# An attention-and-gated-projection kernel whose instruction order a planner makes: new planner costs, an exclusion rule for VectorE and GpSimd, and a longer chosen list

## The chip, the cores and the metric

One core of one Trainium2 chip runs the whole problem in one launch. The metric is the time of one execution on the device, in microseconds, median of the runs shown. Five instruction queues matter: TensorE (PE, with its weight loads PEld), VectorE (DVE), ScalarE (ACT), GpSimd (POOL) and SyncE (SP), which here issues nearly all DMA transfers.

## What is computed

```python
def _attn_ref(q, k, v, omega):                  # q, k, v: 8 x 8 x 576 x 64, omega: 128 x 64
    scale = 1.0 / np.sqrt(np.sqrt(D))
    def phi(x):
        proj = np.einsum('bhsd,md->bhsm', x, omega)
        h = proj - np.sum(x * x, axis=-1, keepdims=True) / 2.0
        return np.exp(h - np.max(h, axis=-1, keepdims=True)) / np.sqrt(m)
    q_p, k_p = phi(q * scale), phi(k * scale)
    kv, z = np.einsum('bhsm,bhsd->bhmd', k_p, v), np.sum(k_p, axis=2)
    num = np.einsum('bhsm,bhmd->bhsd', q_p, kv)
    return num / (np.einsum('bhsm,bhm->bhs', q_p, z)[..., None] + 1e-06)

def _moe_ref(x, w_a, w_b, w_out):               # 4608 x 512, 512 x 1536 twice, 1536 x 512
    return ((x @ w_a) * (x @ w_b)) @ w_out      # x is the attention's output, heads side by side
```

## The kernel before

**Two kinds of work.** Attention is cut into 32 units, one for each batch entry and pair of heads. A unit multiplies its input X by omega (`four`, `eight`: PE lines L583, L603), takes row maxima on DVE (L654, L613), makes biases of them (L661, L662), runs exponentials on ACT (L667, L623), and then forms k'v (pkv), the normaliser and the result. The dense part runs in nine blocks of 512 tokens; its matmuls are written as three products of a high and a low half of each operand, so every operand is first split: a CAST makes the high half, a subtraction (`subber`, L408) the low one. Blocks 0 and 1 (`moe_block`, PE lines L1285 and L1093) use the weights as they are. From block 2 on (`moe_block7`, L1383) a form with seven products in place of eight is used; it needs sums of the weights (`weight_sums`, L1317 to L1326, on DVE).

**The first 300 us carry everything that happens once.** The inputs of the weights come as 64-bit numbers. Each of 36 pieces (`raw`) is turned into a 32-bit number by two ACT instructions (L450, L452) and one DVE instruction (L454), and then split by a CAST, which the planner may give to ACT or to DVE (`convert`), and a DVE subtraction. In the same stretch the first eight attention units run. The first four have a longer way of their own (`tok_tail`): transposes on PE (pq, L990), the products pkv (L1013) and pn (L1027), then on DVE rd (L1032, L1034), x32t (L1035) and tails (L1039), then transposes back on PE (px, L1046; pt, L1050), and a split into the x that the dense blocks read.

**GpSimd** sums the exponentials of a unit over the tokens (`z_sums`, L829: z and zs), in three pairs of additions per unit. DVE transposes and reduces the sums, SP takes them through DRAM into zb, and DVE divides (L895 to L907).

**What sets the order.** Nothing of it is written by hand. Each piece is a `g.op` with its engine or engines, a cost in ns, what it reads and writes, and a priority. `Graph.plan` replays the program by these costs with `run`, which each time starts the piece that can start first. From a replay `dues` works back to the latest time for each piece; the next replay takes DVE, ACT and POOL work by those due times. `CHOSEN` is a list of lists of seeds: in each replay `shifted` adds random delays, drawn from the seed that stands for that 15 us stretch (0: none), to the due times. The order of the last replay is the program's: five queues, each served strictly in order, and a choice of ACT or DVE for some copies. The planner's constants of interest: `BW` and `LANDING` give a transfer's time, `TURNS` the cost of PE changing between kinds of matmul, `PORT` lets half of the time that a DVE piece shares with GpSimd count as lost. `SP` issues cost 330 ns each.

Of the kernel before, what the change touches and what calls it, by code (L numbers as in the profile page):

```python
# [41 lines left out]
CFG = dict(PORT=0.5, EDF=("DVE", "ACT", "POOL"), STEP=15000, LOOK=60000, NOISE=(200, 600), CHOSEN=((448364,600862,0,0,820305,0,0,230255),), ZS=800, ZB=(300, 1600, 3600), ZD=(300, 1600, 3100), HQ=(1100, 2600, 3600), BACK2=(300, 1100, 2600), TW=(), XL=["v0", "v1", "Xt0", "ht2", "hq0"], OWR=["raw0", "raw1"], ONE=((7, 1),), SAFE=500, OWN=16, OWNU=(), HOLD=1000, TG=1, G4=4, WAIT=150, RAW=600, FAST=(0, 1, 2, 3), JOIN0=False, WARM=8, HROOM=["w0", "u1", "w1", "u2", "w2", "u3"], H=3, TURN=(7,), BACK=1500, AT=2, GATES=(-4, -1, 2, 5), SQPE=4, MARGIN=1200, LOAD=1100, SUMS=1000, NATS=(1, 2, 3), CONV=(28000, 2600))  # L42
# [19 lines left out]
class Graph:  # L62
# [3 lines left out]
    BW, LANDING = 330.0, 3400  # L66
    TURNS = {"fr": 190, "rf": 205, "fc": 145, "cf": 205, "rc": 250, "cr": 250}
# [13 lines left out]
    def op(self, eng, fn, r=(), w=(), prio=0, alloc=(), deps=(), margin=0, nbytes=0, at=0, land=0, late=(), fill=False, mode="f"):  # L81
# [5 lines left out]
        o.port = not any(b.ring in ("at", "ab", "o") for b, _ in r)  # L87
# [97 lines left out]
    def begin(self):  # L185
# [17 lines left out]
        self.ready, self.done, self.mode = {e: [] for e in self.ENGINES}, [], "f"  # L203
# [4 lines left out]
    def enter(self, o):  # L208

        t = 0  # L210
        for d in o.deps:
            same = d.eng.keys() == o.eng.keys() == {"PE"}
            t = max(t, d.start + 1, d.end + (0 if same else self.LAT + (150 if "PE" in d.eng else 0)) + (o.land or CFG["SAFE"] * (not o.margin) if d.bytes else 0) - (900 if o.late and o.late is not True and d in o.late else 0))
        o.need = max(t + o.margin, o.at)
        for e in o.eng:
            self.ready[e].append(o)

    def keep(self):

        return (len(self.done), dict(self.free), self.dma_free, list(self.left), {e: list(r) for e, r in self.ready.items()},  # L220
                {n: r["at"] for n, r in self.rings.items()}, dict(self.slots), self.mode)

    def back(self, kept):

        n, free, self.dma_free, left, ready, at, slots, self.mode = kept
# [4 lines left out]
        for name, k in at.items():  # L230
            self.rings[name]["at"] = k

    def run(self, until=1e12, due=None):

        free, ready, found = self.free, self.ready, {}
        while len(self.done) < len(self.ops):
            best = None
            for e in self.ENGINES:
                mine = None
                for o in ready[e]:  # L240
# [114 lines left out]
def pool2(n):  # L355
    return 250 + 2.19 * n
# [3 lines left out]
def tile_attention_moe(ctx: ExitStack, tc: tile.TileContext, kqt, kqtt, kqn, kqnt, vx, omst, idn, wab, wout, out):  # L360
# [69 lines left out]
    g.op({"PE": 2600}, nothing, r=[(zero, None)], w=[(none, None)], alloc=[none], prio=-6000)  # L430
# [37 lines left out]
    for n, (kind, i, w) in enumerate(units):  # L468
# [4 lines left out]
        g.op({"SP": 330}, dma(lambda raw=raw: raw.ap[:], lambda src=src: src), w=[(raw, None)], alloc=[raw], prio=pr - 600,  # L473
# [1136 lines left out]
```

## Time and profile before

| what | value |
|---|---|
| median of 3 runs | 1040.24 us (1039.75 to 1040.35) |
| profiled execution | 1038.92 us, its span 1037.1 us |
| PE busy | 1020.0 us (98%) |
| DVE, ACT, POOL busy | 803.8, 635.5, 117.2 us |
| TensorE clock granted | 0.999 of full speed over the span |
| DMA | 314.39 MB, mean 303 GB/s |

The span is cut into stages by what the program does: up to 50 us the first four attention units, to 300 us dense blocks 0 and 1 with all conversions, then the blocks of seven products. Busy time of PE counts from a matmul's start to its modelled end, and matmuls overlap: twelve of 128x512 follow each other about 0.23 us apart while each is listed at about 0.4 us. A pause of PE under some 0.16 us is therefore not seen as idle time.

### The profile page before, as it was taken

Reading aid. Unit: us, or ns where it says so; the run is one execution under the profiler, and the core shown is the slowest. Engines: PE = TensorE matmul, PEld = TensorE weight load, DVE = VectorE, ACT = ScalarE, POOL = GpSimd, SP = SyncE. Lnnn points to the kernel's source line nnn. Section 1 sums busy time; section 2 is a strip of 40 time slices with the busy share of each in tenths; the row PEclk is TensorE's granted clock in tenths of the full one; section 3 lists DMA queues with packets and bytes.
Section 4 is the critical chain, followed back from the end, with each engine's and each line's share of the span. In section 5 each row is a group of like instructions: output and inputs, shape, how many; then the busy total and the mean of one; then the engine's idle time right before and its main releaser. Section 6 shows DMA issues by size and latency. Waiting matters only on the chain.

```text
span 1037.1 us, 25617 instructions
## 1 busy us (share of the span) xinstructions
PE 1020.0 (98%) x9902; PEld 895.7 (86%) x9902; DVE 803.8 (78%) x1580; ACT 635.5 (61%) x1690; POOL 117.2 (11%) x181
## 2 busy tenths in 40 slices
PE   8899999999999999999999999999999999999998
PEld 6677777777788898989898889988989899999997
DVE  6999999999987687676776868677757467887545
ACT  7998787777676575667556666675555234444322
POOL 0133111111111111110201111111110000000000
PEclk9999999999999999999999999999999999999999
DMA  9977878999889898879898998988798899999991
GB/s 358 335 250 247 291 236 266 323 335 332 292 296 387 301 319 299 319 278 368 283 321 301 340 304 296 363 287 315 249 303 265 267 316 337 334 326 358 338 336 56
DMA packets 123658, 314.39 MB, mean 303 GB/s; under 512 B 17680, under 2 KB 40976, under 8 KB 123536
## 3 DMA queue, kind: packets, MB, share of 16 engines
q1 hardware_dynamic: 122656, 312.10, 86.6%
q8 instruction: 78, 1.28, 0.5%
q10 hardware_dynamic: 880, 0.66, 0.2%
q14 instruction: 44, 0.36, 0.1%
HBM read 255.52 MB, written 57.18 MB: 302 GB/s over the span
## 4 chain that ended last, share of the span: by engine, by line
PE 82%; DVE 12%; ACT 4%; issue 1%; DMA 1%; SPq 0%; DVEq 0%; ACTq 0%
PE p L1383 41%; PE o L1093 19%; PE o_P L1163 5%; PE pa L1285 3%; PE pb L1285 3%; PE pkv L876 3%; PE pm L950 2%; DVE sm L654 2%; PE ppk L603 2%; PE p L603 1%; DVE raw L454 1%; PE p L1163 1%; ACT hq L667 1%; DMA zb<-zdr 1%; ACT hk L667 1%
## 5 line engine op out<-in xcount | busy, mean ns | idle before, releaser
L1093 PE MATMUL o<-wo,ghl 128*128 128x512 f32 x1008 | 263.2, 396 | 0.4 <-DVE ghl L408 0.4
L1093 PEld LDWEIGHTS o<-wo,ghl 128*128 128x128 f32 x1008 | 178.6, 188 | 36.3 <-issue 4.1
L400 ACT COPY c<-p 128x512 f32<-128x512 f32 x150 | 87.4, 583 | 145.7 <-PE p L1383 137.8
L1395 DVE TENSOR_TENSOR c<-p,c 128x512 f32<-128x512 f32 x144 | 98.6, 685 | 71.1 <-PE p L1383 36.4
L1383 PE MATMUL p<-Sa,t 128*128 128x256 f32 x1008 | 133.4, 280 | 0.0
L1383 PEld LDWEIGHTS p<-Sa,t 128*128 128x128 f32 x1008 | 126.2, 188 | 2.3 <-issue 0.2
L829 POOL TENSOR_TENSOR z<-hk 128x256 f32<-128x256 f32 x56 | 48.0, 856 | 601.4 <-ACT hk L623 402.8
L1459 DVE TENSOR_TENSOR c<-c 128x512 f32<-128x512 f32 x82 | 57.8, 707 | 40.1 <-ACT c L400 39.4
L911 ACT ACTIVATE hq<-hq,dn 128x128 f32<-128x128 f32 x224 | 69.3, 390 | 13.5 <-DVE dn L907 13.0
L1285 PE MATMUL pa<-x,wa 128*128 128x512 f32 x288 | 74.4, 400 | 2.1 <-ACT a L400 1.1
L1285 PE MATMUL pb<-x,wb 128*128 128x512 f32 x288 | 72.3, 397 | 1.5 <-DVE a L1293 1.5
L1383 PE MATMUL p<-x,wa 128*128 128x256 f32 x504 | 73.7, 282 | 0.0
L1383 PE MATMUL p<-x,wb 128*128 128x256 f32 x504 | 73.2, 281 | 0.0
L1383 PEld LDWEIGHTS p<-x,wa 128*128 128x128 f32 x504 | 67.2, 188 | 3.3 <-ACT hk L400 0.6
L1383 PE MATMUL p<-Sb,t 128*128 128x256 f32 x504 | 68.4, 283 | 0.0
L1383 PEld LDWEIGHTS p<-x,t 128*128 128x128 f32 x504 | 64.7, 189 | 2.6
L1285 PEld LDWEIGHTS pa<-x,wa 128*128 128x128 f32 x288 | 52.6, 188 | 16.4 <-ACT a L400 1.9
L1383 PE MATMUL p<-Sb,bq 128*128 128x256 f32 x504 | 66.8, 282 | 0.0
L1285 PEld LDWEIGHTS pb<-x,wb 128*128 128x128 f32 x288 | 53.3, 188 | 15.5 <-DVE a L1293 2.8
L1383 PE MATMUL p<-x,t 128*128 128x256 f32 x504 | 66.7, 281 | 0.0
L1383 PEld LDWEIGHTS p<-Sb,bq 128*128 128x128 f32 x504 | 64.3, 189 | 2.4
L1383 PEld LDWEIGHTS p<-x,wb 128*128 128x128 f32 x504 | 65.4, 188 | 0.1
(217 smaller groups left out, 1983.9 us busy)
## 6 DMA issues: line engine op xcount, KB each, us to landing
t<-td SPq DMA_DIRECT2D x168, 512.0 KB
wo<-wod SPq DMA_DIRECT2D x96, 512.0 KB
bq<-bd SPq DMA_DIRECT2D x84, 256.0 KB
qdr<-qd SPq DMA_DIRECT2D x112, 160.0 KB
hq<-qdr SPq DMA_DIRECT2D x28, 640.0 KB
X<-in_kqt_dram SPq DMA_DIRECT2D x30, 512.0 KB
raw<-in_wab_dram SPq DMA_DIRECT2D x24, 512.0 KB
td<-ts SPq DMA_DIRECT2D x24, 512.0 KB
```

The source lines that it names most:

```text
L400: nc.scalar.copy(o(), i())
L603: nc.tensor.matmul(flat[c // 4][w]()[half, c % 4 * M:c % 4 * M + M], x()[rows, c * P + D * t:c * P + D * t + D], om.ap[rows], start=True, ...
L654: g.op({"DVE": dve(4 * M)}, lambda e, w=w, whole=whole: nc.vector.tensor_reduce(sm.ap[:, 0, w, sl], whole(), axis=X, op=ALU.max), r=held[w ...
L829: g.op({"POOL": pool2(n)}, lambda e: nc.gpsimd.tensor_tensor(o(), a(), c(), op=ALU.add), r=r, w=w, alloc=list(al), prio=pri, deps=zload[-1 ...
L876: nc.tensor.matmul(pkv.ap[D * j + d:D * j + d + Q, 0:M], vb.ap[:, vc, d:d + Q], c(), start=(n == 0), stop=(n == 4))
L911: g.op({"ACT": 392}, lambda e, c=c, src=src: nc.scalar.activation(hq.ap[:, c], src(), AF.Copy, scale=dn.ap[:, c:c + 1]), r=[sd, (dn, None) ...
L1093: nc.tensor.matmul(po.ap[:], ghl.ap[:, gi, t * P:(t + 1) * P], wo.ap[:, wi], start=(n == 0 and i == 0), stop=(n == NF - 1 and i == 2))
L1163: nc.tensor.matmul(pb.ap[:, t], A[0](ai)[:, t * P:(t + 1) * P], W[0](wi), start=begin and t == j == 0, stop=stop and t == 1 and j == 2)
L1285: nc.tensor.matmul(pb.ap[:], wt.ap[:, wi, c], xs[c].at(xi), start=(c == 0 and i == 0), stop=(c == NC4 - 1 and i == 2))
L1383: nc.tensor.matmul(pb.ap[:, w], W[w][0](wi, c), X[0](xi, c), start=fresh and n == w == 0, stop=n == 5, skip_group_check=True)
L1395: g.op({"DVE": dve(SM)}, lambda e: nc.vector.tensor_tensor(o.ap[:, q], pb.ap[:], C[y[0]].ap[:, y[1]], op=ALU.add), r=[(pb, 0), (pb, 1), (C ...
L1459: g.op({"DVE": dve(SM)}, lambda e, c=C[k]: nc.vector.tensor_tensor(c.ap[:, :, 1], c.ap[:, :, 1], c.ap[:, :, 0], op=ALU.mult), r=part, w=pa ...
```

## The change

No arithmetic is added or dropped, and every piece stays as it was, except that the two DVE instructions of rd become one piece of the planner. What changes is the planner:

- a DVE piece and a GpSimd piece now exclude each other: one that starts while the other engine holds the `lock` ends a whole duration (less `HOLD`) after the lock is released, on both engines. Pieces that only reduce or transpose (`port=False`) or read PSUM take no part. Before, DVE alone paid, half of the overlap.
- a transfer isn't issued while the modelled backlog is over `DEPTH` = 5600 ns; bandwidth is 395 instead of 330 bytes per ns, the fixed part 1000 + 1500 ns instead of 3400, an SP issue 450 ns instead of 330.
- `TURNS` are about half of what they were; a kind "h" (pkv and pn of the first units) is added.
- `CHOSEN` has six lists in place of one: five empty ones (five replays by due times without delays) and one of 38 entries, 10 of them not 0.

```diff
-CFG = dict(PORT=0.5, EDF=("DVE", "ACT", "POOL"), STEP=15000, LOOK=60000, NOISE=(200, 600), CHOSEN=((448364,600862,0,0,820305,0,0,230255),), ZS=800, ZB=(300, 1600, 3600), ZD=(300, 1600, 3100), HQ=(1100, 2600, 3600), BACK2=(300, 1100, 2600), TW=(), XL=["v0", "v1", "Xt0", "ht2", "hq0"], OWR=["raw0", "raw1"], ONE=((7, 1),), SAFE=500, OWN=16, OWNU=(), HOLD=1000, TG=1, G4=4, WAIT=150, RAW=600, FAST=(0, 1, 2, 3), JOIN0=False, WARM=8, HROOM=["w0", "u1", "w1", "u2", "w2", "u3"], H=3, TURN=(7,), BACK=1500, AT=2, GATES=(-4, -1, 2, 5), SQPE=4, MARGIN=1200, LOAD=1100, SUMS=1000, NATS=(1, 2, 3), CONV=(28000, 2600))
+CFG = dict(EDF=("DVE", "ACT", "POOL"), STEP=15000, LOOK=60000, NOISE=(200, 600), CHOSEN=((),(),(),(),(),(408745,0,244407,0,423927,388522,0,0,0,0,792291,441366,0,0,0,109497,0,0,0,0,41968,0,0,0,0,0,0,0,0,0,0,257791)), ZS=800, ZB=(300, 1600, 3600), ZD=(300, 1600, 3100), HQ=(1100, 2600, 3600), BACK2=(300, 1100, 2600), TW=(), XL=["v0", "v1", "Xt0", "ht2", "hq0"], OWR=["raw0", "raw1"], ONE=((7, 1),), SAFE=500, OWN=16, OWNU=(), HOLD=1000, TG=1, G4=4, WAIT=150, RAW=600, FAST=(0, 1, 2, 3), JOIN0=False, WARM=8, HROOM=["w0", "u1", "w1", "u2", "w2", "u3"], H=3, TURN=(7,), BACK=1500, AT=2, GATES=(-4, -1, 2, 5), SQPE=4, MARGIN=1200, LOAD=1100, SUMS=1000, NATS=(1, 2, 3), CONV=(28000, 2600))
...
-    BW, LANDING = 330.0, 3400
-    TURNS = {"fr": 190, "rf": 205, "fc": 145, "cf": 205, "rc": 250, "cr": 250}
+    BW, LEAD, LANDING, DEPTH, HOLD = 395.0, 1000, 1500, 5600, 130
+    TURNS = {"fr": 90, "rf": 95, "fc": 90, "cf": 75, "rc": 150, "cr": 150, "fh": 95, "hf": 100, "rh": 150, "hr": 100, "hc": 120, "ch": 120}
...
-        o.port = not any(b.ring in ("at", "ab", "o") for b, _ in r)
+        o.port = port and not any(b.ring in ("at", "ab", "o") for b, _ in r)
+        if not o.port and "ACT" in eng and any(b.ring in ("at", "ab", "o") for b, _ in r):
+            o.any = eng = dict(eng, ACT=eng["ACT"] - 30)
...
                     need = o.need if due is None else o.need + due[len(self.ops) + o.n]
+                    if o.bytes:
+                        need = max(need, self.dma_free - self.DEPTH)
...
-                begin = max(s, self.dma_free)
-                self.dma_free = begin + o.bytes / self.BW
+                begin = max(s + self.LEAD, self.dma_free)
+                self.dma_free = begin + max(60, o.bytes / self.BW) + (440 if o.eng[e] > 1000 else 0)
...
                 if e == "DVE" and o.port:
-                    o.end += CFG["PORT"] * max(0, min(o.end, free["POOL"]) - s)
+                    if s < self.lock["POOL"]:
+                        o.end = max(o.end, self.lock["POOL"] + o.eng[e] - self.HOLD)
+                    self.lock["DVE"] = o.end
+                elif e == "POOL":
+                    if s < self.lock["DVE"]:
+                        o.end = max(o.end, self.lock["DVE"] + o.eng[e] - self.HOLD)
+                    self.lock["POOL"] = o.end
...
-        g.op({"SP": 330}, dma(lambda raw=raw: raw.ap[:], lambda src=src: src), w=[(raw, None)], alloc=[raw], prio=pr - 600,
+        g.op({"SP": 450}, dma(lambda raw=raw: raw.ap[:], lambda src=src: src), w=[(raw, None)], alloc=[raw], prio=pr - 600,
...
-            g.op({"DVE": 150}, lambda e, o=o, pn=pn, rd=rd: nc.vector.tensor_scalar(rd.ap[:], pn.ap[:, :, o + D], EPS, None, op0=ALU.add),
-                 r=[(pn, None)], w=[(rd, None)], prio=pri)
-            g.op({"DVE": 165}, lambda e, rd=rd: nc.vector.reciprocal(rd.ap[:], rd.ap[:]), r=[(rd, None)], w=[(rd, None)], prio=pri)
+            def inv(e, pn=pn, rd=rd):
+                nc.vector.tensor_scalar(rd.ap[:], pn.ap[:, :, D], EPS, None, op0=ALU.add)
+                nc.vector.reciprocal(rd.ap[:], rd.ap[:])
+            g.op({"DVE": 470}, inv, r=[(pn, None)], w=[(rd, None)], prio=pri)
```

Lines of the changed kernel lie up to 11 below those of the kernel before (L654 is L665, L400 is L411, L1046 is L1057).

The first place is the head of DVE's queue: the maxima of the first three groups of unit 0 (sm, sme), out of ppk and ppq, and the biases made of them with the sums ps and pse that PE forms. Before:

```order
L654 TENSOR_REDUCE sm_0_183<-ppk_00_179 128x4
L654 TENSOR_REDUCE sm_0_183<-ppq_00_180 128x4
L654 TENSOR_REDUCE sme_0_212<-ppke_00_208 128x4
L654 TENSOR_REDUCE sme_0_212<-ppqe_00_209 128x4
L654 TENSOR_REDUCE sm_0_183<-ppk_04_239 128x4
L661 SCALAR_TENSOR_TENSOR sm_0_183<-sm_0_183,ps_00_265 128x2x4
L662 SCALAR_TENSOR_TENSOR sm_0_183<-ps_00_265,sm_0_183 128x2x4
```

And in the changed kernel:

```order
L665 TENSOR_REDUCE sm_0_169<-ppk_00_165 128x4
L665 TENSOR_REDUCE sm_0_169<-ppq_00_166 128x4
L672 SCALAR_TENSOR_TENSOR sm_0_169<-sm_0_169,ps_00_194 128x2x4
L673 SCALAR_TENSOR_TENSOR sm_0_169<-ps_00_194,sm_0_169 128x2x4
L665 TENSOR_REDUCE sme_0_211<-ppke_00_207 128x4
```

The first pair of biases moved ahead of three maxima. On PE the sums ps_00 moved likewise, to directly behind the first pp group; the next two sums (pse, ps_04) moved behind the pp group of unit 1.

The second place is PE's queue between pn and px of unit 1 (px_1), some 30 us into the program, where px waits for DVE's x32t. Before:

```order
L1027 MATMUL pn_11_652<-kvz_1_532,qT_1_564 64x66 x10
L990 MATMUL pq_20_669<-ident,hq_2_401 128x128 x3
L1013 MATMUL pkv_2_677<-v_2_169,hk_2_400 64x66 x8
L1013 MATMUL pkv_2_677<-v_2_169,htk_0_210 64x66 x2
L1013 MATMUL pkv_2_677<-v_2_169,hk_2_400 64x66 x8
L1013 MATMUL pkv_2_677<-v_2_169,htk_0_210 64x66 x2
L1046 MATMUL px_1_708<-ident,x32t_1_635 128x128 x4
```

And in the changed kernel:

```order
L1038 MATMUL pn_11_643<-kvz_1_523,qT_1_431 64x66 x10
L1024 MATMUL pkv_2_659<-v_2_199,hk_2_404 64x66 x8
L1024 MATMUL pkv_2_659<-v_2_199,htk_0_209 64x66 x2
L1024 MATMUL pkv_2_659<-v_2_199,hk_2_404 64x66 x8
L1024 MATMUL pkv_2_659<-v_2_199,htk_0_209 64x66 x2
L1001 MATMUL pq_20_693<-ident,hq_2_405 128x128 x3
L1061 MATMUL pt_1_698<-ident,tails_1_516 128x128
L1001 MATMUL pq_21_707<-ident,hq_2_405 128x128
L1001 MATMUL pq_21_707<-ident,htq_0_210 128x128
L1001 MATMUL pq_21_707<-ident,hq_2_405 128x128
L1001 MATMUL pq_22_713<-ident,hq_2_405 128x128 x3
L1038 MATMUL pn_20_726<-kvz_2_660,qT_2_694 64x66 x10
```

Behind these stands px_1 (x4): seven transposes and pn_20 of unit 2 moved between pn_11 and px_1.

The third place is ACT's queue ahead of the first copy of pa (a_0) of dense block 0. Before:

```order
L667 ACTIVATE hk_0_913<-ppqk_00_912,smk_0_914 128x128 x3
L400 COPY a_0_860<-pa_0_859 128x512
L450 ACTIVATE raw_520<-raw_520 128x512
L452 ACTIVATE raw_520<-raw_520 128x512
L400 CAST wo_1041<-raw_419 128x512
L400 CAST wa_1048<-raw_495 128x512
```

And in the changed kernel:

```order
L411 CAST wa_1035<-raw_470 128x512
L862 COPY zq_0_1030<-zq_0_1030 32x8 x3
L411 COPY k_1_0_1006<-pkv_0_1005 128x128
L411 CAST wb_1043<-raw_498 128x512
L461 ACTIVATE raw_552<-raw_552 128x512
L463 ACTIVATE raw_552<-raw_552 128x512
L463 ACTIVATE raw_519<-raw_519 128x512
L411 COPY a_0_950<-pa_0_949 128x512
```

Casts of weights and pieces of the second batch entry's first unit moved ahead of a_0. Over the whole program ACT's queue gains 19 copies and DVE's loses as many: 12 casts of weights net in the first 170 us, 8 net of 29 casts of ghl from c after 300 us, one output copy, and 2 casts of ghl from a the other way.

## Rows read from the trace of the kernel before

**Rows 1.** The page: busy time of each engine in us (share of the span, instructions), and the granted TensorE clock in 40 slices of the span, in tenths of full speed (9 is 90% or more).

```profile
PE 1020.0 (98%) x9902; PEld 895.7 (86%) x9902; DVE 803.8 (78%) x1580; ACT 635.5 (61%) x1690; POOL 117.2 (11%) x181
...
PEclk9999999999999999999999999999999999999999
```

**Rows 2.** Windows of the span, from and to in us: the length, then busy us of PE, PEld, DVE, ACT and POOL (with instructions), the granted clock, the busy share of the DMA engines and GB/s.

```profile
0.00:8.85 8.85, 7.85 (x120) 5.46 (x120) 3.53 (x9) 3.18 (x5) 0.94 (x10) 1.00 0.74 257
8.85:25.00 16.15, 13.62 (x283) 11.08 (x282) 12.95 (x35) 16.15 (x58) 0.20 (x1) 1.00 1.04 412
25.00:50.00 25.00, 20.19 (x351) 16.45 (x350) 24.09 (x62) 24.24 (x68) 1.55 (x3) 1.00 0.94 345
50.00:100.00 50.00, 48.92 (x410) 37.56 (x409) 49.51 (x98) 45.85 (x114) 18.06 (x18) 1.00 0.74 241
100.00:200.00 100.00, 98.47 (x853) 75.19 (x855) 97.93 (x198) 79.42 (x219) 18.62 (x24) 1.00 0.84 281
200.00:300.00 100.00, 98.91 (x899) 76.52 (x892) 96.76 (x186) 72.39 (x195) 16.00 (x24) 1.00 0.94 320
300.00:1025.00 725.00, 725.00 (x6945) 666.55 (x6946) 513.58 (x989) 394.25 (x1037) 61.87 (x102) 1.00 0.88 308
1025.00:1037.10 12.10, 7.05 (x60) 6.85 (x58) 5.43 (x9) 0.00 (x0) 0.00 (x0) 0.90 0.29 87
```

**Rows 3.** Whom PE waited for in the whole span, the five largest: us in total, times, the longest.

```profile
PE px L1046 <- DVE x32t L1035: 3.3, 4, 1.4
PE pb L1285 <- DVE a L1293: 1.5, 3, 0.6
PE pq L990 <- DVE rd L1032: 1.1, 1, 1.1
PE pa L1285 <- ACT a L400: 1.1, 2, 0.9
PE none L429 <- DVE zero L422: 1.0, 1, 1.0
```

**Rows 4.** The longest pieces of the chain that ended last (start and duration in us, what, its count).

```profile
89.48 2.79 PE pb L1285 x12
```

**Rows 5.** ACT in order of time, 0 to 12 us: start and duration in us, instruction, count, and in brackets the idle time before it and what ended it.

```profile
5.67 0.63 ACT L638 ACTIVATE x<-X 128x512 f32<-128x512 f32 x1 [0.16 <-DMA X<-in_kqt_dram]
8.85 1.14 ACT L667 ACTIVATE hk<-ppk,sm 128x128 f32<-128x128 f32 x4 [2.55 <-DVE sm L662]
```

**Rows 6.** DVE in order of time, 0 to 12 us, same columns.

```profile
6.60 0.68 DVE L654 TENSOR_REDUCE sme<-ppke 128x4 f32<-128x512 f32 x1
...
8.39 0.15 DVE L661 SCALAR_TENSOR_TENSOR sm<-sm,ps 128x8 f32<-128x8 f32 x1
```

**Rows 7.** PE in order of time, 0 to 12.5 us, same columns: the sums ps for the first group.

```profile
7.02 1.16 PE L643 MATMUL ps<-ind,x 128*128 128x128 f32 x8
```

**Rows 8.** The chain that ended last, in order of time, 0 to 60 us: four exponentials of a unit on ACT.

```profile
11.03 1.03 ACT hk L667 x4
```

**Rows 9.** PE in order of time, 26 to 48 us, same columns: pn of unit 1, transposes, and px of units 1 to 3 with their waits.

```profile
27.06 1.45 PE L1027 MATMUL pn<-kvz,qT 128*64 128x66 f32 x40
...
30.96 0.63 PE L1046 MATMUL px<-ident,x32t 128*128 128x128 f32 x4 [0.66 <-DVE x32t L1035]
...
31.53 0.27 PE L990 MATMUL pq<-ident,hq 128*128 128x128 f32 x1
31.64 0.27 PE L990 MATMUL pq<-ident,htq 128*128 128x128 f32 x1
...
37.09 0.66 PE L1046 MATMUL px<-ident,x32t 128*128 128x128 f32 x4 [1.11 <-DVE x32t L1035]
...
44.80 0.66 PE L1046 MATMUL px<-ident,x32t 128*128 128x128 f32 x4 [1.37 <-DVE x32t L1035]
```

**Rows 10.** DVE instructions that write or read wb: count, then shortest, median and longest in ns, first and last start in us, forms.

```profile
L402 DVE CAST wb<-raw x11: 410/420/964, 38.5 to 162.9; 128x512 fp32r<-128x512 f32 x11
```

**Rows 11.** ACT instructions that write or read wo, same columns.

```profile
L400 ACT CAST wo<-raw x8: 657/663/773, 52.1 to 168.7; 128x512 fp32r<-128x512 f32 x8
```

**Rows 12.** Line L454 of DVE (two inputs in SBUF), same columns.

```profile
L454 DVE SCALAR_TENSOR_TENSOR raw<-raw x36: 639/685/1611, 34.2 to 167.0; 128x512 int32<-128x512 int32 x36
```

**Rows 13.** Line L569 of DVE (a reduction, one input), same columns.

```profile
L569 DVE TENSOR_REDUCE sq<-natk x30: 630/678/687, 14.4 to 695.3; 128x8 f32<-128x512 f32 x30
```

**Rows 14.** Groups of DVE instructions from 50 to 250 us: count, then busy us and mean ns of one, then idle us before them.

```profile
L454 DVE SCALAR_TENSOR_TENSOR raw<-raw 128x512 int32<-128x512 int32 x31 | 23.4, 765 | 0.0
```

**Rows 15.** Groups of POOL instructions from 50 to 250 us, same columns.

```profile
L829 POOL TENSOR_TENSOR z<-hk 128x256 f32<-128x256 f32 x18 | 18.3, 1015 | 143.6 <-ACT hk L667 105.4 <-ACT hk L623 17.5 <-DVE wa L408 14.0
```

**Rows 16.** Line L829 of POOL over the whole span: count, then shortest, median and longest in ns, first and last start in us, forms.

```profile
L829 POOL TENSOR_TENSOR z<-hk x56: 722/742/2672, 49.5 to 770.5; 128x256 f32<-128x256 f32 x56
```

**Rows 17.** PE in order of time around an attention visit of the later stage: the last dense matmuls ahead of it, and the first matmul of the visit.

```profile
311.30 0.86 PE L1093 MATMUL o<-wo,ghl 128*128 128x512 f32 x3
312.09 0.32 PE L603 MATMUL ppk<-om,X 64*64 64x128 f32 x1
```

**Rows 18.** The page, costliest groups: the scalings of a unit by its divisor on ACT (count, busy us, mean ns).

```profile
L911 ACT ACTIVATE hq<-hq,dn 128x128 f32<-128x128 f32 x224 | 69.3, 390 | 13.5 <-DVE dn L907 13.0
```

More of the change, by code (lines that the diff above doesn't have):

```diff
@@ L79, in buf, with op @@
         return b
-    def op(self, eng, fn, r=(), w=(), prio=0, alloc=(), deps=(), margin=0, nbytes=0, at=0, land=0, late=(), fill=False, mode="f"):
+    def op(self, eng, fn, r=(), w=(), prio=0, alloc=(), deps=(), margin=0, nbytes=0, at=0, land=0, late=(), fill=False, mode="f", port=True):
         o = Op()
@@ L202, in begin @@
         self.free, self.dma_free = dict.fromkeys(self.ENGINES, 0), 0
-        self.ready, self.done, self.mode = {e: [] for e in self.ENGINES}, [], "f"
+        self.ready, self.done, self.mode, self.lock = {e: [] for e in self.ENGINES}, [], "f", {"DVE": 0, "POOL": 0}
         for o in self.ops:
@@ L212, in enter @@
             same = d.eng.keys() == o.eng.keys() == {"PE"}
-            t = max(t, d.start + 1, d.end + (0 if same else self.LAT + (150 if "PE" in d.eng else 0)) + (o.land or CFG["SAFE"] * (not o.margin) if d.bytes else 0) - (900 if o.late and o.late is not True and d in o.late else 0))
+            t = max(t, d.start + 1, d.end + (0 if same else self.LAT + (150 if "PE" in d.eng else 40 if "ACT" in d.eng else 0)) + (o.land or CFG["SAFE"] * (not o.margin) if d.bytes else 0) - (900 if o.late and o.late is not True and d in o.late else 0))
         o.need = max(t + o.margin, o.at)
@@ L220, in keep @@
         return (len(self.done), dict(self.free), self.dma_free, list(self.left), {e: list(r) for e, r in self.ready.items()},
-                {n: r["at"] for n, r in self.rings.items()}, dict(self.slots), self.mode)
+                {n: r["at"] for n, r in self.rings.items()}, dict(self.slots), self.mode, dict(self.lock))
     def back(self, kept):
-        n, free, self.dma_free, left, ready, at, slots, self.mode = kept
+        n, free, self.dma_free, left, ready, at, slots, self.mode, lock = kept
         for o in self.done[n:]:
@@ L355, in pool2 @@
 def pool2(n):
-    return 250 + 2.19 * n
+    return 180 + 2.19 * n
 @with_exitstack
@@ L429, in nothing @@
             nc.tensor.matmul(none.ap[:], zero.ap[:], zero.ap[:, 0:1].to_broadcast([P, SM]), start=True, stop=True)
-    g.op({"PE": 2600}, nothing, r=[(zero, None)], w=[(none, None)], alloc=[none], prio=-6000)
+    g.op({"PE": 3250}, nothing, r=[(zero, None)], w=[(none, None)], alloc=[none], prio=-6000)
     for b, src in ((om, omst), (ident, idn)):
@@ L570, in total @@
                 if "POOL" in s.eng:
-                    nc.gpsimd.tensor_scalar(o(), o(), SQ2, 0.0, op0=ALU.mult, op1=ALU.add)
-            g.op({"DVE": dve(n * D)}, total, r=[(nat, None)], w=[(sq, part)], alloc=[sq] if part in (0, None) else [], prio=pr)
+                    nc.vector.tensor_scalar(o(), o(), SQ2, None, op0=ALU.mult)
+            g.op({"DVE": dve(n * D)}, total, r=[(nat, None)], w=[(sq, part)], alloc=[sq] if part in (0, None) else [], prio=pr, port=False)
     def four(nm, b, pri, x, xdep, dst, c0, sm, sq, al, deps, mg, more):
@@ L918, in turn @@
         g.op({"DVE": dve(NCH * M)}, lambda e: nc.vector.transpose(qd.ap[:, :, 0:NCH], hq.ap[:, 0:NCH].rearrange("p c (j r) -> p j c r", r=32)),
-             r=[(hq, c) for c in range(NCH)], w=[(qd, 0)], prio=pr + 110)
+             r=[(hq, c) for c in range(NCH)], w=[(qd, 0)], prio=pr + 110, port=False)
         if u == NU - 1:
```

86 lines of the change are left out of this document (43 added, 43 removed).

## The prediction

> **What bounds the kernel now.** The page comes first: PE is busy 98% of the span at full clock [rows 1]. So the question is where the missing part lies, and that the windows tell [rows 2]. From 300 to 1025 us PE is busy for every microsecond. Up to 300 us it isn't. Idle time there, length less PE's busy time: 1.0 us up to 8.85 us (the start of the program [rows 3]), 2.5 us from 8.85 to 25, 4.8 us from 25 to 50, and 1.1 + 1.5 + 1.1 = 3.7 us from 50 to 300. The last window holds another 5 us, the end of the program. The change can't shorten the matmuls, and their number stays, so an order can win the 2.5 + 4.8 = 7.3 us of the first stage, the 3.7 us of the second, and pauses that the busy time hides. Those are short: twelve matmuls of 128x512 take 2.79 us, 0.23 each [rows 4], while one is listed at 0.86 - 2 x 0.23 = 0.40 us [rows 17], so a pause under 0.17 us never shows. I bound them by as much again as the visible 3.7 us.
>
> The same windows tell which engine holds PE up. From 8.85 to 25 us ACT has no idle time at all (16.15 of 16.15), and from 25 to 50 it has 0.8 us. From 50 to 300 us DVE is busy 244.2 of 250 us, ACT much less from 100 us on [rows 2]. The waits agree: PE's largest is px for DVE's x32t, 3.3 us in four waits, all in the first 50 us, then pb for a product of DVE [rows 3]. So the first stage is ACT's and DVE's, the second DVE's, the third PE's own.
>
> **The change part by part.** The number of instructions is the same but for copies that change engine. Three stages follow.
>
> *Head (0 to 12 us).* ACT waits 2.55 us for the first biases before its first exponential at 8.85 us [rows 5]. DVE makes the biases at 8.39, behind five maxima; the third of these starts at 6.60 [rows 6]. The new order puts the biases there, two maxima in. They also need the sums ps, which PE now forms directly behind the first group; ps and its like take some 1.0 us (eight records, 7.02 to the next group at 8.02 with 1.16 listed [rows 7]) and can start when ACT's first square is done, so 6.6 us holds. The first exponential comes about 8.85 - (8.39 - 6.60) = 7.06 us, 1.8 us earlier. Since ACT then works without a gap up to 25 us, what it starts earlier it ends earlier. But the other two sums now stand behind the group of unit 1 on PE, about 1 us later than before; ACT's queue has squares to fill that time and may still run dry for some of it. Bounds 0 and 1.8; I take 1.0, the 1.8 less the wait for those sums.
>
> *px (15 to 46 us).* The waits of px 1 to 3 show 0.66, 1.11 and 1.37 us [rows 9]. The new order puts more work in front of px. For px_1 that is seven transposes at 0.11 us (two successive starts, 31.53 and 31.64) and one pn of ten, about half of 1.45 us [rows 9]: 0.8 + 0.6 = 1.4 us, over the 0.66 that it waited. For px_2 a group of 16 moves in front, some 1 us, against 1.11; for px_3 half a block's pa (six matmuls at 0.23 us [rows 4]), 1.4 us, against 1.37. All of the 3.3 us is then covered on PE, if x32t comes no later. But it comes from DVE, which this stage keeps full (24.09 of 25 us [rows 2]), and work filled in here must find its own inputs ready. Bounds 0 and 3.3; I take 2.0, nearer to the covered side, because filler was found for each wait.
>
> *Dense blocks 0 and 1 (50 to 300 us).* In the weights' conversions 12 casts move from DVE to ACT and in the products 2 move back, 10 net. A cast takes DVE 0.42 us [rows 10]: 4.2 us of its 244.2 [rows 2]. ACT takes 0.66 us for one [rows 11], 6.6 us in all, and has 50.0 - 45.85 = 4.2 us free from 50 to 100 us, over 20 us in the next 100 [rows 2]. DVE also loses time beside GpSimd: L454, which reads two inputs in SBUF, takes 685 ns at the median, up to 1611 [rows 12], and 765 on the mean between 50 and 250 us [rows 14], so 31 x 80 ns = 2.5 us are lost on that line alone. GpSimd pays too: 1015 ns for an addition there [rows 15] against a median of 742 [rows 16]. A reduction of DVE is never above 687 ns [rows 13]. With 4.2 us off a full engine and PE waiting 3.7 us plus hidden pauses, bounds are 0 and 7.4 us; I take 3.0, most of what is visible, since the casts alone exceed it.
>
> The Trainium skill ("SBUF — State Buffer", Who interferes with whom) says that an instruction of VectorE with two inputs in SBUF and a GpSimd one exclude each other, whichever comes first holding the other up for its whole length, and that a reduction never takes part on trn2. The rows on L454, L569 and GpSimd agree, and it is the rule that the new planner follows where the old one charged half. By it an order with reductions beside the additions would lose nothing there, PE's 3.7 visible us would all go, and the time would be 0.7 us lower than my sum; an order that only lets GpSimd lose instead would give the sum itself.
>
> *Changes of PE's kind of work.* Counted in the two orders, 168 become 172. One costs about 0.1 us: the visit's first matmul starts 0.79 us after the first of three dense ones, whose own time is 3 x 0.23 = 0.70 [rows 17]. That adds 0.4 us. The third stage keeps its order nearly everywhere and PE its full load [rows 2]: 0 us, at most a pause of a few tenths. The bounded backlog and the new costs of transfers only move issues in SP's queue; up to the 19th transfer that queue reads as before, and no wait of PE for a transfer is among its largest [rows 3], so 0 us. The end of the program is unchanged.
>
> Sum: -1.0 - 2.0 - 3.0 + 0.4 = -5.6 us. The profiled execution took 1038.92 us (span 1037.1), so 1033.3; the median of the runs lies 1.3 us above that execution, so **1034.6 us**.
>
> **The rivals.**
>
> *All of it goes.* DVE, relieved, lets PE run through; the first stage's 7.3 us lose the 1.8 + 3.3 that I bounded, the second its 3.7 and 2 more of hidden pauses: -10.8 + 0.4, 1029.8 us. For it speaks that DVE is so full [rows 2] that its relief might carry over to each wait; against it, that px's waits are of a chain through DVE and ACT, not of PE's order alone.
>
> *The waits only move.* In the first stage ACT and DVE have no room; filling PE's queue in front of px doesn't make x32t come earlier, the pieces pulled in front lack their inputs, and each wait reappears one instruction on. The relief of DVE is used up by pieces of attention that were pulled ahead. Then the time is 1040.2 + 0.4 - the head's 1.0, about 1039.6, no change. For it: ACT's 16.15 of 16.15 us.
>
> *ACT becomes what bounds 50 to 100 us: slower.* Counted in the orders, 32 more ACT instructions stand ahead of its third copy of pa (204 against 172): 16 exponentials at 0.26 us [rows 8], 9 scalings at 69.3 / 224 = 0.31 us [rows 18], 2 casts at 0.66 us [rows 11], and five small copies, some 0.2 us each: 4.2 + 2.8 + 1.3 + 1.0 = 9.3 us. ACT has 4.2 us free from 50 to 100 us and 0.8 before [rows 2], and the head gives it 1.0. So the third step of the dense block starts up to 9.3 - 6.0 = 3.3 us later, and the matmuls of a copied step queue behind on PE. The attention work pulled ahead is PE's too and fills some of it. If it fills none and nothing is made up, the 3.3 stand in place of the second stage's gain, and with px's gain lost as well: 1040.2 + 3.3 + 0.4 - 1.0 = 1042.9. It decides from the point at which ACT's queue, not DVE's, is the last that pa waits for; before, that wait is 1.1 us in two [rows 3].
>
> **How the numbers follow.** The forecast, with each of its terms somewhere within its bounds (1031 to 1038): 0.52. All of it goes (1027 to 1031, its 1029.8 with hidden pauses of 1 to 5 us in place of 2): 0.18. The waits only move (1038.2 to 1042.3): 0.15. ACT bounds (over 1042.3): 0.15. The measurement tells about 0.2%, 2.1 us, from no change. Faster: 0.52 + 0.18 = 0.70; same 0.15; slower 0.15. The range reaches from 1027.0, the lower end of the case in which all of it goes, to 1042.3, and leaves out the last rival.
>
> **What would show it.** Head: the first exponential of ACT at about 7 us in place of 8.85. px: its waits for x32t gone or under 1 us in all, and PE's idle time from 8.85 to 50 us down from 7.3 to about 4.5. Second stage: DVE's busy time from 50 to 300 us down by 4 us or more, PE's idle time from 3.7 to about 1, L454's mean nearer to 685. Third stage: PE busy 725 of 725 still. The prediction is wrong if ACT shows no idle time from 50 to 100 us and PE's waits for ACT's a grow, if a wait of PE or ACT for a DMA appears among the largest, or if PE idles after 300 us.

## The result and the profile after

| | before | after |
|---|---|---|
| median of 6 runs each | 1039.73 us (1038.62 to 1040.35) | 1045.53 us (1044.80 to 1046.07) |
| ratio, 95% interval | | 1.0056 (1.0044 to 1.0069) |
| span of the profiled execution | 1037.1 us | 1044.3 us |

The change makes the kernel slower by 0.56%, where some 0.5% faster was forecast. The profiled executions lie further apart than the medians, 7.15 us in place of 5.8: 1038.92 us before, and 1046.07 after, the slowest of its six. What follows is read from these two. The first view to read is the same as before the prediction: the page's engine line, the clock, and the windows of the span (columns as in [rows 2]).

```profile
PE 1025.9 (98%) x9902; PEld 898.4 (86%) x9902; DVE 794.9 (76%) x1561; ACT 645.5 (62%) x1709; POOL 111.8 (11%) x181
...
PEclk9989999999999999999999999999999999999999
```

```profile
8.85:25.00 16.15, 14.71 (x296) 12.05 (x288) 13.78 (x36) 15.33 (x52) 0.20 (x1) 1.00 1.04 404
25.00:50.00 25.00, 20.62 (x410) 16.71 (x410) 23.25 (x63) 24.66 (x73) 4.04 (x8) 1.00 0.85 306
50.00:100.00 50.00, 47.78 (x404) 36.36 (x405) 46.62 (x94) 47.40 (x122) 9.71 (x12) 0.93 0.76 236
100.00:150.00 50.00, 49.25 (x433) 37.04 (x432) 45.35 (x92) 42.72 (x112) 9.64 (x12) 1.00 0.73 248
150.00:200.00 50.00, 50.00 (x440) 38.56 (x442) 45.51 (x90) 41.52 (x110) 9.45 (x12) 1.00 0.94 309
200.00:250.00 50.00, 50.00 (x405) 39.52 (x394) 47.77 (x97) 39.16 (x107) 9.33 (x12) 1.00 0.94 325
250.00:300.00 50.00, 49.21 (x368) 38.86 (x368) 47.68 (x90) 31.49 (x82) 5.88 (x10) 1.00 0.90 321
300.00:1025.00 725.00, 722.38 (x6942) 660.34 (x6941) 513.35 (x982) 396.85 (x1044) 62.56 (x105) 1.00 0.89 310
```

Three things differ from [rows 2]. PE's idle time up to 50 us is 1.44 + 4.38 = 5.8 us, down from 7.3. From 50 to 300 us it is 3.76 us in all, against 3.7, though DVE has 244.2 - 232.9 = 11.3 us less to do; 2.2 us of it lie before 100 us, where the clock fell as well. And after 300 us PE, which had no idle microsecond, now has 2.6.

How late PE is can be read from one instruction that stands in both queues: the first matmul of the attention visit of [rows 17], which started at 312.09 us, and the last group of all. That group in the kernel before, PE in order of time:

```profile
1030.46 1.60 PE L1163 MATMUL o_P<-wo,ghl 128*128 128x256 f32 x12
```

And both in the changed kernel:

```profile
314.11 0.32 PE L614 MATMUL ppk<-om,X 64*64 64x128 f32 x1
...
1037.49 1.59 PE L1174 MATMUL o_P<-wo,ghl 128*128 128x256 f32 x12
```

At that visit PE starts 2.02 us later than before, and three matmuls of o (0.7 us) that were then done are still to come: 2.7 us behind. At the end it is 7.03 us behind. So the first 312 us lose 2.7 us and the rest 4.3, in place of 5.6 won and nothing. The waits of PE name the culprit in each part (columns as in [rows 3]):

```profile
PE ppq L594 <- ACT k L411: 2.4, 1, 2.4
PE p L1394 <- ACT c L411: 2.2, 4, 1.4
PE px L1057 <- DVE rd L1043: 1.1, 1, 1.1
...
PE pb L1296 <- ACT a L411: 0.7, 1, 0.7
```

Both large ones are for copies on ACT. PE's four waits for px (3.3 us in [rows 3]) are down to one of 1.1.

**After 300 us.** The waits of ACT hold a line that the kernel before has at 1.8 us in that stretch, and the instructions of the tiles natk and natq (inputs of an attention unit, 256 KB each, which ACT squares in place) show how often it stood from 280 us on: first the line of the whole span, then natk's and natq's.

```profile
ACT natk L575 <- DMA natk<-in_kqn_dram: 13.6, 12, 2.7
```

```profile
L575 ACT ACTIVATE natk<-natk x15: 630/632/663, 302.3 to 696.7; 128x512 f32<-128x512 f32 x15
its engine sat idle before it (us, times) until:
  DMA natk<-in_kqn_dram: 11.3, 9
```

```profile
L575 ACT ACTIVATE natq<-natq x17: 615/632/657, 289.2 to 713.7; 128x512 f32<-128x512 f32 x17
...
  DMA natq<-in_kqn_dram: 7.9, 4
```

19.2 us in 13 waits, against 3.1 in four for the same tiles before. Here is the largest, in order of time: SP's queue, then ACT's, then PE's.

```profile
629.64 1.04 SPq L422 DMA_DIRECT2D t<-td  x2
630.89 0.33 SPq L422 DMA_DIRECT2D natk<-in_kqn_dram  x1
```

```profile
633.59 2.45 ACT L634 ACTIVATE hq<-hq,sm 128x128 f32<-128x128 f32 x8
638.75 0.63 ACT L575 ACTIVATE natk<-natk 128x512 f32<-128x512 f32 x1 [2.71 <-DMA natk<-in_kqn_dram]
...
641.32 0.66 ACT L575 ACTIVATE natq<-natq 128x512 f32<-128x512 f32 x1
641.85 0.60 ACT L411 COPY c<-p 128x512 f32<-128x512 f32 x1
```

```profile
640.27 0.87 PE L1394 MATMUL p<-x,wb 128*128 128x256 f32 x6
642.50 0.75 PE L1394 MATMUL p<-Sa,t 128*128 128x256 f32 x4 [1.37 <-ACT c L411]
```

natk is issued at 630.89, behind two t, and ACT can't square it until 638.75, 7.9 us later. ACT stands for 2.71 us of these, works without a gap through what has piled up, and copies c out of p at 641.85; PE has had no free p since its last group and stands for 1.37 us. The planner had counted on less: by the constants in the diff a load of 262144 bytes with nothing ahead of it was taken to land 262144 / 330 + 3400 = 4194 ns after its issue, and now 1000 + 262144 / 395 + 1500 = 3164 ns. With what stands ahead of them in the plan, these loads land 4.5 us after issue at the median in the changed kernel's plan (6.9 with the old transfer costs in the new planner, experiment 3). The square may follow 1.1 us later (`LOAD`, 1100 ns, the same in both kernels).

**Around 50 us.** ACT in order of time, ahead of the copy of k for which PE waits, and PE:

```profile
48.31 0.75 ACT L461 ACTIVATE raw<-raw 128x512 f32<-128x512 f32 x1
48.89 0.74 ACT L463 ACTIVATE raw<-raw 128x512 int32<-128x512 uint32 x1
49.48 0.68 ACT L461 ACTIVATE raw<-raw 128x512 f32<-128x512 f32 x1
50.04 0.67 ACT L411 CAST wa<-raw 128x512 fp32r<-128x512 f32 x1
50.73 0.61 ACT L862 COPY zq<-zq 32x8 f32<-32x8 f32 x3
51.24 0.25 ACT L411 COPY k<-pkv 128x128 f32<-128x128 f32 x1
```

```profile
48.41 0.40 PE L887 MATMUL pkv<-htk,v 128*32 128x128 f32 x8
48.74 0.43 PE L594 MATMUL ppk<-om,X 64*64 64x128 f32 x2
51.55 0.32 PE L594 MATMUL ppq<-om,X 64*64 64x128 f32 x1 [2.38 <-ACT k L411]
```

pkv is ready at 48.8 us; three pieces of weight conversion, a cast and zq stand ahead of its copy in a full ACT queue. Behind this wait the granted clock fell to 0.50, the lower of its two levels, for 6.6 us:

```profile
51.50:53.00 1.50, 1.45 (x32) 1.24 (x33) 1.45 (x5) 1.48 (x3) 0.00 (x0) 1.00 0.63 240
53.00:59.60 6.60, 5.93 (x15) 3.93 (x13) 4.56 (x10) 5.96 (x17) 1.78 (x3) 0.50 0.79 206
```

### The profile page after: what moved, and what is told of

Its sections match the earlier page's. It is cut to its first block, busy times and chain, and to the rows that moved or that the text cites. A ratio compares the mean times of both kernels' runs of the same rounds, so it can differ in the third digit from the quotient of the medians.

```text
span 1044.3 us, 25595 instructions
## 1 busy us (share of the span) xinstructions
PE 1025.9 (98%) x9902; PEld 898.4 (86%) x9902; DVE 794.9 (76%) x1561; ACT 645.5 (62%) x1709; POOL 111.8 (11%) x181
## 4 chain that ended last, share of the span: by engine, by line
PE 74%; DVE 10%; DMA 7%; ACT 6%; issue 1%; SPq 0%; DVEq 0%; ACTq 0%
PE p L1394 36%; PE o L1104 17%; PE o_P L1174 4%; PE pb L1296 3%; DMA natk<-in_kqn_dram 3%; PE pa L1296 3%; PE pkv L887 2%; PE pm L961 2%; PE ppk L614 2%; PE p L614 1%; PE ppk L594 1%; DMA raw<-in_wout_dram 1%; PE p L1174 1%; DVE sm L624 1%; DVE raw L465 1%
## 5 line engine op out<-in xcount | busy, mean ns | idle before, releaser
L411 ACT COPY c<-p 128x512 f32<-128x512 f32 x150 | 87.5, 583 | 172.6 <-PE p L1394 161.3
```

Of the source, the lines that this page charges most:

```text
L411: nc.scalar.copy(o(), i())
```

## The experiments

Theory 1: the new costs of transfers let the planner put each square on ACT ahead of its data; the copies that PE needs stand behind it. Theory 2, for the first stage: PE loses there by the order of ACT's queue. Where a kernel keeps an order, the planner runs as it did, and its finished list is then sorted by changed keys; engines not named keep their queues row for row. The change also prices some other pieces anew that its list leaves out (a square on ACT 25 ns more, a GpSimd addition 70 ns less, new figures for pkv, pn and the products of the divisor); none of these was tried alone.

**1. The squares 4 us later.** Only ACT's queue changes, in 33 places.

```diff
+        key = {o: o.start for o in self.order}
+        for o in self.order:
+            if o.start > 280000 and "ACT" in o.eng and any(d.bytes and d.alloc and d.alloc[0].name.startswith("nat") for d in o.deps):
+                key[o] = max(o.start, min([o.start + 4000, *(x.start - 900 for x in self.after[o])]))
+        self.order.sort(key=lambda o: (key[o], o.n))
```

> The changed kernel with its planned order, in which only 33 squares of ACT (natk, natq, natee after 280 us) stand up to 4 us later in ACT's queue, 1 to 12 rows back; the queues of PE, DVE, GpSimd and SP are row for row the changed kernel's. Theory 1 (the new costs of transfers let the planner put each square behind a transfer that has not landed; ACT stands, and the copies of p that PE needs stand behind it): ACT's idle time ahead of squares after 280 us falls from 23.6 us to under 5, PE's loss after 300 us falls by 3.5 to 5 us, about 1041 us. Rival A (those waits of ACT lie beside other waits and cost PE nothing; the loss is of the extra casts on ACT or of the orders picked): the waits fall likewise, the time stays within 1 us of 1045.5.

1042.55 us (1040.28 to 1045.06, 10 runs; 1.0028 of before, 1.0018 to 1.0037): 3.0 us of the 5.8 are back. The clock doesn't explain it: among the runs with a mean granted clock of 0.999 or 1.0 the medians are 1045.2 us for the changed kernel (two runs) and 1042.0 here (five), among the others 1045.6 (four) and 1042.9 (five). ACT has no wait left for natk or natq. The two instructions named above, in its trace:

```profile
311.88 0.32 PE L619 MATMUL ppk<-om,X 64*64 64x128 f32 x1
...
1032.00 1.59 PE L1179 MATMUL o_P<-wo,ghl 128*128 128x256 f32 x12
```

From the visit on PE loses 1.54 - (-0.21) - 0.7 = 1.05 us against before, where the changed kernel lost 4.3: 3.3 us are of the squares. Theory 1 holds, with 3.3 us where it expected 3.5 to 5; the median is 1.5 us above its forecast, while the profiled execution (1040.89 us) met it. Its runs differ by 4.8 us, more than those of the kernel before (below).

**2. The reverse, on the kernel before.** Its squares stand up to 3 us further ahead in ACT's queue.

```diff
+            d = [d for d in o.deps if d.bytes and d.alloc and d.alloc[0].name.startswith("nat")]
+            if o.start > 280000 and "ACT" in o.eng and d:
+                key[o] = max(d[0].start + 1, o.start - 3000)
```

> The kernel before with its own order, in which only the squares of ACT after 280 us stand up to 3 us further ahead in ACT's queue; the other four queues are untouched. Theory 1: ACT's idle time ahead of squares after 280 us goes from 4.4 us to 10 or more, PE waits for ACT's c, and the time goes from 1039.7 to 1041.5 to 1044. Rival A (ACT's waits for transfers cost PE nothing): the waits grow likewise, the time stays within 0.7 us of 1039.7.

1051.75 us (1050.71 to 1052.78; 1.0115, 1.0100 to 1.0130). ACT's waits for natk and natq are 13.9 and 6.4 us, nearly the changed kernel's, and they cost far more than forecast. Its largest waits of PE:

```profile
PE p L1389 <- ACT c L406: 5.3, 8, 1.5
...
PE p L1389 <- ACT hq L406: 1.3, 1, 1.3
```

The two instructions again:

```profile
314.51 0.32 PE L609 MATMUL ppk<-om,X 64*64 64x128 f32 x1
...
1042.21 1.60 PE L1169 MATMUL o_P<-wo,ghl 128*128 128x256 f32 x12
```

PE is 2.42 us late at the visit and 11.75 at the end, so 9.3 us are lost behind the visit. (At least 1.1 of the 2.42 are not the edit's: PE idles 2.1 us from 150 to 200 us, where the queues are unchanged, in place of 1.0.) So theory 1 is shown from both sides: in a kept order, squares that stand ahead of their data cost PE time, and the same squares further back give it back. What a wait of ACT costs PE depends on what stands behind it: about 20 us of waits cost 3.3 us in one order and 9.3 in the other.

**3. The cost model alone, planned anew.** Three kernels change constants of the changed planner, one drops its seeds. The lines are cut to what changes; in the first kernel the bound and the lead also go from the code.

```diff
-    BW, LEAD, LANDING, DEPTH, HOLD = 395.0, 1000, 1500, 5600, 130
+    BW, LANDING, HOLD = 330.0, 3400, 130
...
+    BW, LEAD, LANDING, DEPTH, HOLD = 395.0, 1000, 1500, 10 ** 9, 130
...
-LOAD=1100
+LOAD=4100
...
-CHOSEN=((),(),(),(),(),(408745,0,244407,
+CHOSEN=((),(),(),(),(),())
```

> The changed kernel with the transfer model of the kernel before (330 bytes per ns, 3400 ns fixed, no bound on the backlog; SP's issues still 450 ns); all orders are planned anew. Theory 1: the planned landing of the nat loads goes from 4.5 to 6.9 us after issue at the median, ACT's waits for them after 280 us fall below 8 us, and the time falls to 1038 to 1042. Rival A (the exclusion rule, the casts on ACT or the replays are at fault): 1044 or more.

> The changed kernel with only the bound on the backlog taken away (DEPTH so large that it never acts); transfers still cost 395 bytes per ns and 1000 + 1500 ns. Planned landing of the nat loads 4.3 us after issue at the median, as short as with the bound. Theory 1: ACT's waits for them stay above 12 us after 280 us and the time stays near 1045, 1043 to 1048. Rival B (the bound holds issues back, and that is why the loads land late): the waits fall below 8 us, 1039 to 1042.

> The changed kernel with one constant changed, LOAD 4100 in place of 1100: the planner expects a nat load 3 us later before it places the square; all else is planned anew. Theory 1: ACT's waits for the nat loads fall below 5 us after 280 us and the time falls by 3 to 5 us, 1040 to 1043. Rival A: within 1 us of 1045.5, apart from what a new order brings by chance.

> The changed kernel with six replays by due times and no random delays (its list of seeds replaced by an empty one). If the list of seeds carries what the new costs are worth: several us over 1045.5, 1048 to 1062 as the other newly planned orders were (1052 to 1062). If any order by the new rules is as good: 1044 to 1047.

| | time | ACT's waits for natk + natq after 280 us | PE idle, 50 to 150 us |
|---|---|---|---|
| before | 1039.7 us | 1.8 + 1.3 us | 1.6 us |
| changed | 1045.5 | 11.3 + 7.9 | 3.0 |
| old transfer costs | 1052.41 | 3.6 + 0 | 4.3 |
| no bound on the backlog | 1062.34 | 15.7 + 7.1 | 8.5 |
| margin of the squares 4100 | 1060.46 | 0 + 0 | 7.8 |
| replays without delays | 1051.05 | 12.3 + 4.5 | 6.1 |

The waits came out as theory 1 expected in each: long where transfers are taken to be short, with the bound or without (rival B falls), short where either constant allows for more. The times didn't: all four are 5 to 17 us above the changed kernel, and all lose part of that in dense blocks 0 and 1 (last column). Nor did PE's waits follow those of ACT. With the margin of 4100 ACT never waits for natk or natq after 280 us, and PE's line for c reads as in the changed kernel:

```profile
PE p L1394 <- ACT c L411: 2.2, 4, 1.1
```

In another order PE waits for c for other reasons, so it is the two experiments with kept orders that carry theory 1. An order planned anew differs everywhere, and the list of seeds (32 numbers, nine of them not 0, and not 38 and ten as the section on the change has it) stands beside one set of constants; with others its orders were worse. Such a run tells nothing on what a constant is worth, only what it does to a wait. The last row shows that without seeds the new rules give 1051 us. All further experiments keep an order.

**4. Around 50 us.** Three kernels, all with the squares 4 us later: two copies ahead in ACT's queue; besides, the low half of x ahead in DVE's; and instead, three casts moved to DVE (wb0 and wb1, which were there before the change, and wa1, which was not).

```diff
+        for at, to in {48778: 46550, 51185: 50080, 48923: 50100, 49489: 50120, 50054: 50140}.items():
+            key[act[at]] = to
...
+        key[next(o for o in self.order if "DVE" in o.eng and round(o.start) == 48612)] = 46200
...
+        for at in (41770, 47743, 48923):
+            act[at].eng = {"DVE": 426}
```

> As the run with the squares 4 us later (1042.55 us), and in ACT's queue two copies stand four rows further ahead: k (of pkv, unit 0 of the second batch entry) ahead of two raw pieces, a cast and zq, and the first a ahead of a cast and three raw pieces. All other queues are the changed kernel's. Theory 2 (between 48 and 60 us PE waits because these copies stand behind work on the weights in a full ACT queue, and the clock falls behind that wait in some executions): PE's waits of 2.4 and 0.9 us there fall below 0.6 together, the granted clock stays at 1.0 from 50 to 60 us, and the time falls to 1039 to 1040.5 us. Rival C (ACT has too much work there whatever its order): PE waits as long for the next product of ACT, 1042 or more.

1043.23 us (1042.23 to 1046.73). The wait for k is gone, and PE stands instead for the low half of x, 1.0 us at 52.15, then 0.7 for a.

> As the run with two copies ahead (1043.23 us), and in DVE's queue the low half of x (unit 3), for which pa then waited 1.0 us, stands four rows further ahead. Theory 2 (PE's waits between 48 and 60 us come of the order of the full queues there): the waits of 1.0 and 0.7 us that were left fall below 0.8 together, the granted clock stays at 1.0 from 50 to 60 us, 1040 to 1041.5 us. Rival C (ACT and DVE are both full there, and a wait taken away comes back at the next product): PE waits as long again behind it, 1042.5 or more.

1042.84 us (1041.91 to 1045.01). That wait is gone too, and the next is as long; the clock falls behind it:

```profile
PE ppk L603 <- DVE raw L474: 2.0, 1, 2.0
```

```profile
54.00:58.00 4.00, 2.03 (x10) 1.34 (x8) 3.97 (x10) 4.00 (x12) 0.00 (x0) 1.00 0.76 212
58.00:62.00 4.00, 4.00 (x37) 3.07 (x38) 3.29 (x9) 4.00 (x11) 2.46 (x3) 0.57 0.77 264
```

> As the run with the squares 4 us later (1042.55 us), and three casts of weights that stand ahead of the first two ACT copies around 50 us (wb0, wa1, wb1) run on DVE, at the same place of the order. Theory 2 in the form that the casts themselves are the load: ACT's copy of k comes 1.1 us earlier, PE's wait for it goes from 2.4 to about 1.3 us, 1041 to 1042 us. Rival D (DVE, which is full from 25 to 50 us too, pays as much): PE waits for DVE instead (px, pt, sm), 1042.5 or more.

1041.16 us (1040.81 to 1042.80, 10 runs; 1.0019, 1.0010 to 1.0028), 1.4 us below the run with the squares alone by the medians, with runs that overlap (1040.28 to 1045.06 there). The time is the one that theory 2 expected of the casts as a load, and below rival D's. But the wait for k is still 2.2 us, not 1.3, so the gain, if there is one, isn't where it was expected; the clock was 0.999 or more over the span in nine of its ten runs. What the three casts are worth stays open. Theory 2 in its first form, the order of the queues, falls: with the waits for k and for x taken away the time is 1042.8 to 1043.2 us and not 1039 to 1041.5. In the windows above DVE is busy 3.97 of 4 us from 54 to 58 and ACT 4.00, and a wait taken away comes back at the next product of either. That is rival C, and the same thing that the prediction named as its second and third rivals.

**5. The relief of DVE.** In the changed kernel with later squares, the casts that it took from DVE after 60 us go back; in the kernel before, 11 such casts go to ACT; and in that last, the head's biases also move ahead.

```diff
+                if o.alloc[0].name in ("wa3", "wa4", "wb4", "wo4", "wa5", "wa6", "wb6", "wb7", "wa8", "wo8", "wa9", "wb9", "wo9", "wb10"):
+                    o.eng = {"DVE": 426}
...
+            if o.alloc and o.alloc[0].name in ("wo4", "wa5", "wa6", "wb6", "wb7", "wa8", "wo8", "wa9", "wb9", "wo9", "wb10"):
+                o.eng = {"ACT": 665}
...
+            if "PE" in o.eng and o.alloc and o.alloc[0].name == "ps_0_00":
+                key[o] = 5843
+            if "DVE" in o.eng and round(o.start) == 9085:
+                key[o] = 6700
```

> As the run with the squares 4 us later (1042.55 us), and the 14 casts of weights after 60 us that the changed kernel took from DVE run on DVE again, two others on ACT as before (net 12), at the same places of the order. If the relief of DVE by casts is what wins 4 us between 100 and 250 us, that gain goes: DVE's busy time there is 4 to 5 us more, PE's loss at 250 us 3 to 4 us more, 1045 to 1047 us. If the gain is of the order (GpSimd's additions beside reductions) and not of the casts: within 1 us of 1042.5.

1044.11 us (1043.01 to 1045.01), 1.6 above its parent by the medians, with runs that overlap, and between the two expectations. From 60 to 250 us DVE is busy 182.29 us against 178.00, as forecast, and PE 187.46 against 189.27, 1.8 us less.

> The kernel before with its own order, in which only 11 casts of weights after 85 us that it gives to DVE (wo4, wa5, wa6, wb6, wb7, wa8, wo8, wa9, wb9, wo9, wb10) run on ACT, at the same places of the order: the copies that change engine, alone. If the relief of DVE is what won time between 100 and 250 us: DVE's busy time there is about 4 us less, PE's loss falls by 1.5 to 3 us, 1036.7 to 1038.2 us. If the gain needs the new order (or ACT's 0.66 us a cast delays the copies of a as much): 1039.0 to 1040.5.

1038.95 us (0.9995, 0.9985 to 1.0005): no change that can be measured. DVE's busy time from 100 to 200 us falls only from 97.93 to 95.97, PE's idle time there from 1.5 to 0.75.

> The run of the kernel before with 11 casts on ACT (1038.95 us), and in its head the sums ps of the first group stand directly behind that group on PE, and the first pair of biases behind two maxima on DVE, as the change has them. If the head's gain carries through to the end: ACT's first exponential at about 7.9 in place of 8.85 us, PE's loss at 25 us 1 us less, 1038.0 us, and 1.6 below the kernel before. If DVE, full until 250 us, takes it back: 1038.7 to 1039.7.

1039.16 us (0.9997, 0.9988 to 1.0006). The first exponential comes at 8.13 us, but ACT then runs dry for 1.43 us at 11.22, and nothing is left at the end. No version here beats the kernel before by more than can be measured.

## Why the prediction was wrong, point by point

- **The step that failed behind the visit at 312 us** is the one that priced transfers at nothing: "The bounded backlog and the new costs of transfers only move issues in SP's queue [...] so 0 us", and with it "The third stage keeps its order nearly everywhere and PE its full load [rows 2]: 0 us". I looked for a wait of PE for a transfer. A planner's cost of a transfer also sets when its *consumer* stands in its queue, and the consumer is ACT, on which PE waits for c. Measured: 4.3 us after the visit at 312 us, 3.3 of them by the squares (experiment 1, and the reverse in experiment 2). The sign that the prediction gave for being wrong, a wait of ACT for a DMA among the largest, is the line that shows it. None of the three rivals had it.
- **The step that failed ahead of the visit** is the sum -1.0 - 2.0 - 3.0: it took each wait that goes as time won at the end, in stages whose own windows show ACT or DVE full. By the forecast PE would have been some 5.6 us ahead at the visit, and it was 2.7 behind: 8.3 us, more than the transfers' 4.3. Without the transfers the forecast would have failed too. PE's visible idle time fell by 1.5 us up to 50 us and not at all from 50 to 300; waits came back at other products of ACT (k and a, below), as experiment 4 shows of waits that are taken away one by one. The rest, 2.7 + 1.5 = 4.2 us, lies in time that counts as busy. In the run with the later squares, whose clock held, it is 0.5 + 2.0 = 2.5 us (its idle time from 8.85 to 300 us is 9.0, before 11.0). The clock's fall is in the first figure; what the second is made of stays open.
- **Head, -1.0:** the first exponential comes at 7.87 us, 0.98 earlier and not 1.8, since DVE's first maximum starts at 6.01 in place of 5.39 us; ACT then ran dry for 0.48 us as feared. PE's idle time from 8.85 to 25 us fell by 1.1. So the local number came right, but by another sum, which is in part luck; alone on the old order the gain doesn't reach the end.
- **px, -2.0:** the waits for px fell from 3.3 to 1.1 us, but PE's idle time up to 50 us only from 7.3 to 5.8, where 4.5 was forecast.
- **Dense blocks, -3.0:** mis-sized. DVE did become free (11.3 us less busy), and from 150 to 250 us PE has no idle time left where it had 1.85 us. But the casts are worth some 1.6 us by the medians of experiment 5 in the new order and at most 1.6 in the old (0.0015 of 1039.6), and PE idles more elsewhere: 2.2 us from 50 to 100 us in place of 1.1, 0.8 from 250 to 300 in place of 0.2.
- **The third rival** came about in its mechanism: ACT, with more conversions ahead of a, became the engine that PE waits for between 48 and 55 us (2.4 us for k, 0.7 for a). It had 0.15 at 1042.9 us. I gave it the price of later copies and left out the clock. In the execution with the later squares, whose clock didn't fall, PE is 0.5 us behind at the visit (0.7 - 0.21); in the changed kernel's, where it did, 2.7. But the clock needn't be all of that difference. The profiled execution of the run with three casts on DVE, with the clock at 1.00 from 50 to 62 us, is 1.76 + 0.7 = 2.5 us behind as well:

```profile
313.85 0.32 PE L622 MATMUL ppk<-om,X 64*64 64x128 f32 x1
```

- **Changes of PE's kind of work, +0.4:** not told apart from the rest in any run.
- **The exclusion rule** brought little that the trace shows: from 50 to 250 us L465 takes 752 ns on the mean against 765 in [rows 14], GpSimd's z 947 against 1015 in [rows 15]. That reductions take no part (the Trainium skill, "SBUF — State Buffer", Who interferes with whom) agrees: L580 never takes more than 687 ns. But additions still last up to 1546 ns, twice their shortest.

What stays open: the run with the later squares has a median 2.9 us above the kernel before and a spread of 4.8 us, while its profiled execution (1040.89 us) lies 1.7 below its median. The clock falls in some of its runs (0.995 to 1.0 over the span) and explains part; a run at 1.0 took 1042.77 us all the same. The rest wasn't traced to one cause beyond the full queues at 50 us.

## What to carry to other kernels

A cost that a planner assigns to a transfer is a promise to the instruction that reads it: before calling such a change free, list the readers, the engine that each stands on, and what is queued behind it there. Where a wait is moved between two engines that are both full, it comes back one product later; count what is added to a stage before pricing the wait that goes. And an order that was searched for belongs to its constants: test a constant by editing the finished order, not by planning anew.

## What the hardware showed

- A load of 256 KB issued among loads of t took 7.9 us from issue to use where ACT waited for it, where the planner counts 3.2 us to the landing with nothing ahead and 4.5 at the median; another (natk, issued at 434.31, squared at 440.95) 6.6 us.
- The clock fell to 0.50 for 6.6 us after an idle time of PE of 2.38 us in one execution, and not after one of 2.40 us at the same place in another (the later squares), whose next windows read 1.00:

```profile
51.50:53.00 1.50, 0.82 (x29) 0.83 (x30) 1.43 (x5) 1.45 (x6) 0.00 (x0) 1.00 0.92 369
53.00:59.60 6.60, 5.74 (x59) 4.07 (x53) 6.53 (x13) 6.60 (x19) 1.69 (x3) 1.00 0.69 195
```
